# Attention and MoE on one core: from tile 16 on, probabilities are transferred into float32r buffers and transposed as float32r

## The chip, the core and the metric

The kernel runs on one core of one Trainium2 chip. A core has TensorE (PE, with its weight loads shown apart as PEld), VectorE (DVE), ScalarE (ACT), GpSimd (POOL) and SyncE (SP), which here only issues DMAs. The metric is the device time of one execution in microseconds; the median of three runs is used.

## What is computed

Attention over a window and some global positions, followed by a feed-forward part with a maximum of three products. All data are float32.

```python
# 8 batches, 8 heads, 512 local and 32 global positions, head size 64
s_g = scale * q_g @ k_all.T                       # global rows see all 544 positions
out_g = sm(s_g) @ v_all
s_ll = where(abs(i - j) <= 32, scale * q_l @ k_l.T, -1e9)
s_l = concat([scale * q_l @ k_g.T, s_ll])         # local rows: global positions and a window
out_l = sm(s_l) @ concat([v_g, v_l])
x = concat([out_g, out_l]) as (8 * 544, 512)
h = maximum(maximum(x @ w1, x @ w2), x @ w3)      # 512 -> 768
out = h @ w_out                                   # 768 -> 512
```

## The kernel before

**Tiles.** Heads go in pairs (4 pairs a batch, 32 in all), and each pair has four tiles of 128 query rows, so 128 tiles; `sl` counts tiles, `p` pairs, `t` is the tile's place in its pair. A tile sees a window of 192 or 224 keys (`WIN`), for the two heads side by side: its probabilities are a buffer of 128 partitions x 2 heads x up to 224 float32.

**One tile.** `scores` (L299) multiplies queries and keys on PE into PSUM, takes mask and minimum on DVE (L320), the exponential on ACT (L322), the reciprocal of the sum on DVE (L324, L325), and scales by it in `times` (L112 on POOL, in most cases), all in place in one buffer: `early[sl % 6]` for tiles 0 to 15, `prob[sl % 4]` from then on (L306). `trans` (L331) transposes the probabilities in four blocks of 128 x 128 on PE (L338), each with a weight load of the probabilities and the identity `ident` as the moving operand, into the PSUM tile `T`; ACT or DVE copy `T` to `pt`. `pv` (L369) multiplies `pt` by the values. The global rows of a pair go through `glob` and `glob_soft`, whose last act is six small DMAs from `sg` into `probg` (L297); `transg` (L352) transposes one block of `probg` per tile (L359).

**Two kinds of arithmetic.** Up to tile 27 (scores) and 25 (values) the matmuls are plain float32. Later ones use float32r operands, each split into a rounded part and a rest (`copy` and `sub`, L102 and L94) and multiplied in parts. Engines that write a float32r buffer round; a DMA moves bytes.

**The MoE part** of batch b - 1 is a generator (`moe_group`, L407) that emits one matmul at a time (L417 for the three products, L436 for the last one). The loop over tiles pulls 18 of them per tile with `fill`, so PE has the feed-forward of one batch between the attention of the next. Its weights are converted from a packed form during the first 26 tiles (`convert`, L155: a DMA into `wraw`, ACT L164, DVE L167 to L170, ACT L177, POOL L181); `WS` says how many steps of that stand in each tile.

**Order.** A tile's `trans` stands one tile ahead of its `pv`, and its `scores` two tiles ahead of its `trans` (L509 and after; further ahead for tiles 0 to 15). A scheduler orders the instructions of each engine from the traced program, with its own estimate of when things are ready; the transposes of tile 16 are the point behind which PE's later instructions are kept (L339 to L341). Which engine takes a copy or a scaling is decided by running sums of costs (`least`, L79). All DMAs are issued by SP in one queue, which waits in order.

**The start.** `ident` is built on POOL (L115); POOL then fills `prob`, `probg`, `qgz` and, last, `early` with zeros (L124 to L132). `early` shares its memory (tag `wol`) with a weight that is written later.

Of the kernel before, what the change touches and what calls it, by code (L numbers as in the profile page):

```python
# [9 lines left out]
F32 = mybir.dt.float32  # L10
F32R = mybir.dt.float32r
# [36 lines left out]
def f32(ap):  # L48
    return ap.bitcast(F32)


def body(ctx, tc, kin, qin, vin, min_, w1, w2, w3, w4, out):
    nc = tc.nc
    act, dve, pool, pe = nc.scalar, nc.vector, nc.gpsimd, nc.tensor

    const = ctx.enter_context(tc.tile_pool(name="const", bufs=1))
    att = ctx.enter_context(tc.tile_pool(name="att", bufs=2))
# [18 lines left out]
    def spend(e, ns):  # L76
        load[e] += ns
# [26 lines left out]
    def times(out, a, col):  # L104
        n = width(out)
        e = least({"d": n * 0.52 + 125, "a": n * 0.833 + 185, "p": n * 1.27 + 150})
        if e == "d":
            dve.tensor_scalar(out=out, in0=a, scalar1=col, scalar2=None, op0=ALU.mult)
        elif e == "a":
            act.activation(out=out, in_=a, func=AF.Copy, scale=col)  # L110
        else:
            pool.tensor_scalar(out=out, in0=a, scalar1=col, scalar2=1.0, op0=ALU.mult, op1=ALU.mult)  # L112

    ident = const.tile([128, 128], F32, name="ident")
    make_identity(nc, ident)  # L115
    mask = const.tile([128, 2, 256], BF16, name="mask")
    zero = small.tile([128, 1], F32, name="zero", bufs=1)
    dve.memset(zero, 0.0)
    prob = [const.tile([128, 2, 256], F32, name=f"prob{i}") for i in range(4)]

    probg = [const.tile([128, 3, 128], F32, name=f"probg{i}") for i in range(2)]

    qgz = const.tile([128, 2, 160], F32R, name="qgz")
    for t in (*prob, *probg):  # L124
        pool.memset(t, 0.0)
    pool.memset(f32(qgz), 0.0)

    wh = [const.tile([128, 3, 4, 128], F32R, name=f"wh{f}") for f in range(6)]
    wl = [const.tile([128, 3, 4, 128], F32R, name=f"wl{f}") for f in range(6)]

    early = const.tile([128, 6, 2, 256], F32, name="early", tag="wol")
    pool.memset(early, 0.0)  # L132
    cut = const.tile([128, 6, 512], I32, name="cut", tag="woh")
    wo = []
    xg = const.tile([128, NP, B, SG], F32, name="xg")
# [73 lines left out]
    EARLY, AHEAD = 16, 9  # L209
    kraw, kst, qraw, qs, vraw, vs, xr, sc, pg, pts = [{} for _ in range(10)]  # L210
# [73 lines left out]
    def glob_soft(p):  # L284
        if p >= B * NP:
            return
        s, nm, z = pg[p]
        dve.tensor_tensor(out=nm[:, 0:1], in0=nm[:, 0:1], in1=nm[:, 1:2], op=ALU.min)
        act.activation(out=s, in_=s, func=AF.Exp, bias=nm[:, 0:1], scale=-1.0, accum_out=z[:, 0:1])
        dve.tensor_scalar(out=z[:, 0:1], in0=z[:, 0:1], scalar1=1e-9, scalar2=None, op0=ALU.add)  # L290
        dve.reciprocal(out=z[:, 0:1], in_=z[:, 0:1])
        spend("d", 220)
        spend("a", 760)
        times(s, s, z[:, 0:1])

        for c0, n, i, h, d0 in GPUT:
            nc.sync.dma_start(out=probg[p % 2][64 * h:64 * h + 64, i, d0:d0 + n], in_=s[:, c0:c0 + n])  # L297

    def scores(sl):  # L299
        if sl >= NS:  # L300
            return
        p, t = divmod(sl, 4)
        c0, n = WIN[t]

        ps = pm.tile([128, 512], F32, name="pm") if sl < 12 else psS.tile([128, 512], F32, name="S")
        s = sc[sl] = early[:, sl % 6] if sl < EARLY else prob[sl % 4]  # L306
        nm = small.tile([128, 2], F32, name="nm")
        z = small.tile([128, 2], F32, name="z")
        ph = [ps[:, 0:224], ps[:, 224:448]]
        for j in range(2):  # L310
            if sl in NATK:

                pe.matmul(ph[j][:, 0:n], lhsT=qraw[sl][:, 128 * j:128 * j + 128], rhs=kraw[p][:, c0:c0 + n],  # L313
                          start=True, stop=True)
                continue
            for a in range(2):
                pe.matmul(ph[j][:, 0:n], lhsT=qs[sl][:, a, 128 * j:128 * j + 128],  # L317
                          rhs=kst[p][:, j, c0:c0 + n], start=(a == 0), stop=(a == 1))
        for j in range(2):
            dve.tensor_tensor_reduce(out=s[:, j, 0:n], in0=ph[j][:, 0:n], in1=mask[:, (1, 0, 1, 0)[t], 32 * (t == 0):32 * (t == 0) + n],  # L320
                                     scale=-0.125, scalar=3.0e38, op0=ALU.add, op1=ALU.min, accum_out=nm[:, j:j + 1])
            act.activation(out=s[:, j, 0:n], in_=s[:, j, 0:n], func=AF.Exp, bias=nm[:, j:j + 1], scale=-1.0,  # L322
                           accum_out=z[:, j:j + 1])
        dve.tensor_scalar(out=z, in0=z, scalar1=1e-9, scalar2=None, op0=ALU.add)  # L324
        dve.reciprocal(out=z, in_=z)  # L325
        for j in range(2):
            times(s[:, j, 0:n], s[:, j, 0:n], z[:, j:j + 1])
        spend("d", 2 * (n * 1.04 + 220) + 440)
        spend("a", 2 * (n * 0.833 + 278))

    def trans(sl):  # L331
        if sl >= NS:
            return
        s = sc.pop(sl)
        ps = psT.tile([128, 512], F32, name="T")
        for j in range(2):
            for c in range(2):
                i = pe.transpose(ps[:, 256 * j + 128 * c:256 * j + 128 * c + 128], s[:, j, 128 * c:128 * c + 128], ident)  # L338
        if sl == EARLY:  # L339

            ctx.enter_context(tc.issue_after(i.ins))  # L341
        src = ps.rearrange("p (x q) -> p x q", q=128)
        if sl < NAT:
            pt = pts[sl] = att.tile([128, 2, 2, 160], F32, name="pt", tag="pt")
            copy(pt.rearrange("p j c q -> p (j c) q")[:, :, 0:128], src, True)
        else:
            pt = pts[sl] = att.tile([128, 2, 2, 2, 160], F32R, name="pt", tag="pt")
            v = pt.rearrange("p j c a q -> p (j c) a q")
            copy(v[:, :, 0, 0:128], src, True)
            sub(v[:, :, 1, 0:128], src, f32(v)[:, :, 0, 0:128], True)  # L350

    def transg(sl):  # L352
        if sl >= NS:
            return
        p, t = divmod(sl, 4)
        pt = pts[sl]
        i, h, n = GCH[t]
        g = psS.tile([128, 512], F32, name="S")
        pe.transpose(g[:, 0:128], probg[p % 2][:, i], ident)  # L359
        src = g[:, 64 * h:64 * h + 64 * n].rearrange("p (c j g) -> p c j g", j=2, g=SG)  # L360
        if sl < NAT:
            copy(pt.rearrange("p j c q -> p c j q")[:, 0:n, :, 128:160], src, True)
            return
        v = pt.rearrange("p j c a q -> p c j a q")
        hi, lo = v[:, 0:n, :, 0, 128:160], v[:, 0:n, :, 1, 128:160]
        copy(hi, src, True)
        sub(lo, src, f32(hi), True)
# [134 lines left out]
    for sl in range(NS):  # L502
        p, t = divmod(sl, 4)
        b, n = divmod(p, NP)
# [23 lines left out]
        if sl % 16 >= 12:  # L528
            i = sl % 16 - 12
# [58 lines left out]
```

## Time and profile before

| | us |
|---|---|
| median of 3 runs | 855.65 |
| lowest and highest | 852.6 and 860.24 |
| the profiled execution | 856.24 |
| its span, first to last instruction | 854.5 |

The profile is of one execution. A span is what the instructions cover; 1.7 us of the execution's time lie around it. Where the profile names a releaser behind "<-", that is the work whose end ended a wait. Durations of PE's matmuls overlap, since they are pipelined: from the start of one to the start of the next is what one costs.

### The profile page before, as it was taken

To read this page: it belongs to the slowest core of one execution; us is meant where nothing else is said; L and a number is where in the kernel's file an instruction comes from. 1 tells how busy PE (TensorE), PEld (TensorE's weight loads), DVE (VectorE), ACT (ScalarE), POOL (GpSimd) and SP (SyncE) were. 2 spreads that over 40 slices of the span, in tenths; PEclk is the share of its full clock that TensorE was granted. 3 is DMA by queue.
4 is the path that set the end of the run, shared out by engine and by line. 5 is a ranking of instruction groups with operands and counts; after the bars stand their busy time and mean duration, and the time that the engine had idled before them with its cause. 6 is when DMAs were issued, how large, how long until landed. Compare 5 with 4: busy or idle time off the path is not lost.

```text
span 854.5 us, 15297 instructions
## 1 busy us (share of the span) xinstructions
PE 815.9 (95%) x4452; PEld 682.8 (80%) x4452; DVE 573.5 (67%) x1783; ACT 529.0 (62%) x1479; POOL 512.5 (60%) x685
## 2 busy tenths in 40 slices
PE   4867979999999999999999999999999999999997
PEld 3644757888888888888888888888888888888896
DVE  4987897676777777766777677777786776421111
ACT  3955566777677676766676776776776675511111
POOL 3865576676677566766677666866676664411211
PEclk8968999999999999999999999999999999999999
DMA  7745553232222322232223222132223211000000
GB/s 221 207 143 147 180 168 106 73 102 78 67 64 74 102 63 60 66 122 71 72 66 102 73 69 68 57 115 61 66 72 121 66 51 32 34 17 1 25 26 25
DMA packets 72420, 71.24 MB, mean 83 GB/s; under 512 B 18960, under 2 KB 63120, under 8 KB 72336
## 3 DMA queue, kind: packets, MB, share of 16 engines
q1 hardware_dynamic: 72336, 70.26, 27.7%
q8 instruction: 36, 0.59, 0.3%
q14 instruction: 48, 0.39, 0.2%
HBM read 56.85 MB, written 8.91 MB: 77 GB/s over the span
## 4 chain that ended last, share of the span: by engine, by line
PE 86%; DVE 7%; DMA 3%; ACT 2%; issue 1%; POOL 0%; SPq 0%; DVEq 0%; ACTq 0%
PE pm L417 46%; PE pm L436 17%; PE O L386 7%; PE T L338 6%; PE S L317 5%; DMA wraw<-w_in 2%; DVE wraw L169 2%; PE S L276 2%; PE S L359 2%; PE pm L313 1%; PE O L379 1%; DVE cut L170 1%; DMA wraw<-wo_in 1%; DVE cut L167 1%; DVE cut L168 1%
## 5 line engine op out<-in xcount | busy, mean ns | idle before, releaser
L417 PE MATMUL pm<-xs,wh 128*128 128x512 f32 (+1 forms) x1296 | 408.9, 388 | 2.2 <-POOL xs L94 2.2
L417 PEld LDWEIGHTS pm<-xs,wh 128*128 128x128 f32 x1296 | 234.0, 190 | 33.8 <-POOL xs L94 2.7
L417 PE MATMUL pm<-xs,wl 128*128 128x512 f32 (+1 forms) x648 | 255.5, 394 | 0.0
L417 PEld LDWEIGHTS pm<-xs,wl 128*128 128x128 f32 x648 | 122.9, 190 | 22.6 <-issue 1.8
L112 POOL TENSOR_SCALAR prob<-prob,z 128x192 f32<-128x192 f32 (+1 forms) x220 | 98.0, 458 | 66.2 <-ACT lox L102 38.2
L436 PE MATMUL pm<-woh,h 128*128 128x512 f32 x408 | 133.5, 398 | 0.0
L94 POOL TENSOR_TENSOR h<-m,h 128x512 fp32r<-128x512 f32 (+1 forms) x54 | 68.3, 1265 | 100.1 <-ACT h L102 100.1
L425 DVE TENSOR_TENSOR m<-pm,m 128x512 f32<-128x512 f32 (+1 forms) x108 | 71.2, 659 | 70.6 <-PE pm L417 69.6
L322 ACT ACTIVATE prob<-prob,nm 128x192 f32<-128x192 f32 (+1 forms) x224 | 103.3, 462 | 16.1 <-DVE nm L320 13.7
L94 POOL TENSOR_TENSOR qs<-qraw,qs 128x256 fp32r<-128x256 f32 x100 | 73.5, 744 | 63.9 <-ACT qs L102 62.5
L94 DVE TENSOR_TENSOR pt<-T,pt 128x512 fp32r<-128x512 f32 x102 | 70.5, 691 | 58.8 <-ACT pt L102 58.0
L324 DVE TENSOR_SCALAR z<-z 128x2 f32<-128x2 f32 x128 | 53.1, 415 | 50.5 <-ACT prob L322 48.7
L436 PEld LDWEIGHTS pm<-woh,h 128*128 128x128 f32 x408 | 74.8, 189 | 11.5
L436 PE MATMUL pm<-wol,h 128*128 128x512 f32 x204 | 82.5, 405 | 0.0
L102 ACT CAST pt<-T 128x512 fp32r<-128x512 f32 x90 | 52.8, 587 | 45.5 <-PE T L338 43.9
L94 POOL TENSOR_TENSOR vs<-vraw,vs 128x256 fp32r<-128x256 f32 x102 | 75.5, 740 | 9.0 <-ACT vs L102 4.8
L320 DVE CUSTOM_DVE_ANT_0 prob<-S,mask 128x192 f32<-128x192 f32 (+1 forms) x224 | 74.8, 371 | 6.7 <-PE S L313 4.1
L94 POOL TENSOR_TENSOR kst<-kraw,kst 64x576 fp32r<-64x576 f32 x49 | 70.5, 1439 | 11.1 <-issue 7.8
L102 ACT CAST qs<-qraw 128x256 fp32r<-128x256 f32 x100 | 40.7, 407 | 55.7 <-PE S L317 54.2
L386 PEld LDWEIGHTS O<-pt,vs 128*128 128x128 f32 x408 | 66.2, 188 | 8.3
L386 PE MATMUL O<-pt,vs 128*128 128x320 f32 (+1 forms) x408 | 72.7, 299 | 0.0
L338 PEld LDWEIGHTS T<-ident,prob 128*128 128x128 f32 x448 | 56.0, 141 | 15.0 <-POOL prob L112 0.2
(99 smaller groups left out, 1351.7 us busy)
## 6 DMA issues: line engine op xcount, KB each, us to landing
vraw<-v_in SPq DMA_DIRECT2D x128, 128.0 KB, 2.1
qraw<-q_in SPq DMA_DIRECT2D x100, 128.0 KB, 2.2
wraw<-w_in SPq DMA_DIRECT2D x18, 512.0 KB, 4.2
out_dram<-o SPq DMA_DIRECT2D x32, 256.0 KB, 2.5
kraw<-k_in SPq DMA_DIRECT2D x25, 320.0 KB, 3.0
qn<-q_in SPq DMA_DIRECT2D x28, 128.0 KB, 2.7
wraw<-wo_in SPq DMA_DIRECT2D x6, 512.0 KB, 3.7
probg<-sg SPq DMA_DIRECT2D x96, 24.0 KB, 1.9
```

Source lines behind the costliest of these rows:

```text
L94: (dve if least(c) == "d" else pool).tensor_tensor(out=out, in0=a, in1=b, op=ALU.subtract)
L102: act.copy(out=out, in_=a)
L112: pool.tensor_scalar(out=out, in0=a, scalar1=col, scalar2=1.0, op0=ALU.mult, op1=ALU.mult)
L317: pe.matmul(ph[j][:, 0:n], lhsT=qs[sl][:, a, 128 * j:128 * j + 128], rhs=kst[p][:, j, c0:c0 + n], start=(a == 0), stop=(a == 1))
L320: dve.tensor_tensor_reduce(out=s[:, j, 0:n], in0=ph[j][:, 0:n], in1=mask[:, (1, 0, 1, 0)[t], 32 * (t == 0):32 * (t == 0) + n], scale=-0.12 ...
L322: act.activation(out=s[:, j, 0:n], in_=s[:, j, 0:n], func=AF.Exp, bias=nm[:, j:j + 1], scale=-1.0, accum_out=z[:, j:j + 1])
L324: dve.tensor_scalar(out=z, in0=z, scalar1=1e-9, scalar2=None, op0=ALU.add)
L338: i = pe.transpose(ps[:, 256 * j + 128 * c:256 * j + 128 * c + 128], s[:, j, 128 * c:128 * c + 128], ident)
L386: pe.matmul(o[:, j, 0:320].rearrange("p (a q) -> p a q", a=2)[:, :, 0:n], lhsT=vs[sl][:, 2 * j + c].rearrange("p a d -> p (a d)"), rhs=pt[ ...
L417: pe.matmul(ps[:, 0:n], lhsT=w[f][:, i, k], rhs=xs[k][:, a, 0:n], start=(q == 0), stop=(q == 11))
L425: dve.tensor_tensor(out=m[:, 0:n], in0=ps[:, 0:n], in1=m[:, 0:n], op=ALU.max)
L436: pe.matmul(ps, lhsT=hh[f][:, a, 128 * t:128 * t + 128], rhs=w[:, f], start=(q == 0), stop=(q == 17))
```

## The change

Three things are changed.

1. From tile 16 on, the softmax of a tile runs in a plain float32 buffer `s` (four of them, in turn). A DMA on SP's queue then moves the scaled probabilities into one of two float32r buffers `prob`. The transposes read `prob` as float32r, with an identity `identr` in float32r, and write a float32r view of the PSUM tile `T`.
2. The global rows' buffers `probg` become float32r, and their 128 transposes too; their DMAs stay as they are. Tiles 0 to 15 still transpose float32 in place.
3. To make room, `ident` moves into the sixth part of `early`, which leaves five parts for the tiles 0 to 15. `early` is now filled with zeros first, and two buffers `prob` in place of four after it. `identr` is a copy of `ident` made by DVE.

```diff
-    ident = const.tile([128, 128], F32, name="ident")
+    early = const.tile([128, 6, 2, 256], F32, name="early", tag="wol")
+    ident = early[:, 5, 0, 0:128]
     make_identity(nc, ident)
+    identr = const.tile([128, 128], F32R, name="identr")
+    dve.tensor_copy(out=identr, in_=ident)
...
-    prob = [const.tile([128, 2, 256], F32, name=f"prob{i}") for i in range(4)]
-    probg = [const.tile([128, 3, 128], F32, name=f"probg{i}") for i in range(2)]
+    prob = [const.tile([128, 2, 256], F32R, name=f"prob{i}") for i in range(2)]
+    probg = [const.tile([128, 3, 128], F32R, name=f"probg{i}") for i in range(2)]
     qgz = const.tile([128, 2, 160], F32R, name="qgz")
-    for t in (*prob, *probg):
-        pool.memset(t, 0.0)
-    pool.memset(f32(qgz), 0.0)
+    pool.memset(early[:, 0:5], 0.0)
+    for t in (*prob, *probg, qgz):
+        pool.memset(f32(t), 0.0)
...
-    early = const.tile([128, 6, 2, 256], F32, name="early", tag="wol")
-    pool.memset(early, 0.0)
...
-        s = sc[sl] = early[:, sl % 6] if sl < EARLY else prob[sl % 4]
+        if sl < EARLY:
+            s = sc[sl] = early[:, sl % 5]
+        else:
+            s = att.tile([128, 2, 224], F32, name="s", bufs=4)
+            sc[sl] = prob[sl % 2]
...
+        if sl >= EARLY:
+            nc.sync.dma_start(out=f32(sc[sl])[:, :, 0:n], in_=s[:, :, 0:n])
...
+        pr, one = (ps, ident) if sl < EARLY else (ps.bitcast(F32R), identr)
         for j in range(2):
             for c in range(2):
-                i = pe.transpose(ps[:, 256 * j + 128 * c:256 * j + 128 * c + 128], s[:, j, 128 * c:128 * c + 128], ident)
+                i = pe.transpose(pr[:, 256 * j + 128 * c:256 * j + 128 * c + 128], s[:, j, 128 * c:128 * c + 128], one)
...
-        pe.transpose(g[:, 0:128], probg[p % 2][:, i], ident)
+        pe.transpose(g.bitcast(F32R)[:, 0:128], probg[p % 2][:, i], identr)
```

The scheduler is given another program, so rows move. Line numbers of the changed kernel are a little higher: L320 becomes L325, L338 becomes L346, L417 becomes L425, and so on; a number behind a name is a buffer's.

PE, in the stretch where a batch's feed-forward runs beside the next batch's attention, around the transposes of one tile with t = 1. Before:

```order
L417 MATMUL pm<-xs,wl_112 128x512
L338 MATMUL T<-ident,prob_93 128x128 x4
L417 MATMUL pm<-xs,wh_107 128x512 x2
L417 MATMUL pm<-xs,wl_113 128x512
L417 MATMUL pm<-xs,wh_107 128x512
L317 MATMUL S<-kst,qs 128x224 x4
```

and after:

```order
L425 MATMUL pm<-xs,wl_111 128x512
L346 MATMUL T<-identr,prob_93 128x128 x4
L425 MATMUL pm<-xs,wh_106 128x512 x2
L425 MATMUL pm<-xs,wl_112 128x512
L425 MATMUL pm<-xs,wh_106 128x512
L322 MATMUL S<-kst,qs 128x224 x4
```

Nothing moved there: four transposes stand between the same matmuls, in another type and from another buffer.

SP's queue in the same stretch, one pair of heads: queries (`qraw`), values (`vraw`), keys (`kraw`) and the six transfers of the global rows. Before:

```order
L297 DMA probg_94<-sg 64x64
L240 DMA qraw<-q_in 128x256
L252 DMA vraw<-v_in 128x256
L240 DMA qraw<-q_in 128x256
L252 DMA vraw<-v_in 128x256 x2
L240 DMA qraw<-q_in 128x256 x2
L252 DMA vraw<-v_in 128x256
L218 DMA kraw<-k_in 128x640
```

and after:

```order
L298 DMA probg_95<-sg 64x64
L241 DMA qraw<-q_in 128x256
L334 DMA prob_93<-s 128x2x224
L253 DMA vraw<-v_in 128x256
L241 DMA qraw<-q_in 128x256
L334 DMA prob_92<-s 128x2x224
L253 DMA vraw<-v_in 128x256
L334 DMA prob_93<-s 128x2x192
L253 DMA vraw<-v_in 128x256
L241 DMA qraw<-q_in 128x256 x2
L334 DMA prob_92<-s 128x2x192
L219 DMA kraw<-k_in 128x640
```

Four transfers a pair have come in, one for each tile; the loads stand among themselves as they did.

DVE, first rows of the program: `mask` is the cast of the mask, L280 the minimum of the global rows, L167 to L169 the first weight conversion, L320 the minimum of a tile. Before:

```order
L484 CAST mask<-cut 128x2x224
L280 ISA sg,nmg<-S,zero 64x384
L280 ISA nmg 64x1
L280 ISA sg,nmg<-S,zero 64x160
L280 ISA nmg 64x1
L288 TENSOR_TENSOR nmg<-nmg 64x1
L290 TENSOR_SCALAR zg<-zg 64x1
L291 RECIPROCAL zg<-zg 64x1
L167 TENSOR_SCALAR cut<-cut 128x512
L168 TENSOR_SCALAR cut<-cut 128x512
L169 SCALAR_TENSOR_TENSOR wraw<-wraw,cut 128x512
L320 ISA early,nm<-pm,mask 128x192
```

and after:

```order
L492 CAST mask<-cut 128x2x224
L281 ISA sg,nmg<-S,zero 64x384
L281 ISA nmg 64x1
L325 ISA early,nm<-pm,mask 128x192
L325 ISA nm 128x1
L325 ISA early,nm<-pm,mask 128x192
L325 ISA nm 128x1
L325 ISA early,nm<-pm,mask 128x224
L325 ISA nm 128x1
L325 ISA early,nm<-pm,mask 128x224
L325 ISA nm 128x1
L281 ISA sg,nmg<-S,zero 64x160
```

The first tiles' minima have moved ahead of the rest of the global rows and of the first weight conversion, which in the changed program stands behind the minima of eight tiles. On PE, ACT, POOL and SP the order differs likewise up to about tile 28; from there on it is the same but for the new transfers and a few swapped neighbours on DVE.

More of the change, by code (lines that the diff above doesn't have):

```diff
@@ L296, in glob_soft @@
         for c0, n, i, h, d0 in GPUT:
-            nc.sync.dma_start(out=probg[p % 2][64 * h:64 * h + 64, i, d0:d0 + n], in_=s[:, c0:c0 + n])
+            nc.sync.dma_start(out=f32(probg[p % 2])[64 * h:64 * h + 64, i, d0:d0 + n], in_=s[:, c0:c0 + n])
     def scores(sl):
```

## The prediction, made before the change was run

> **What bounds the kernel now.** I read the page first (busy time, then the chain that ended last), then the busy time by stage, then the instructions of TensorE (PE) around one tile, and last the first 20 us.
>
> ```profile
> span 854.5 us, 15297 instructions
> PE 815.9 (95%) x4452; PEld 682.8 (80%) x4452; DVE 573.5 (67%) x1783; ACT 529.0 (62%) x1479; POOL 512.5 (60%) x685
> PE 86%; DVE 7%; DMA 3%; ACT 2%; issue 1%; POOL 0%; SPq 0%; DVEq 0%; ACTq 0%
> ...
> 0.00:20.00 20.00, 9.06 (x28) 6.67 (x29) 7.80 (x34) 6.54 (x19) 7.11 (x16) 0.86 0.74 228
> 20.00:149.00 129.00, 106.32 (x600) 78.54 (x599) 110.24 (x296) 86.87 (x249) 88.27 (x96) 0.89 0.53 159
> 149.00:745.00 596.00, 595.81 (x3262) 506.69 (x3263) 438.01 (x1421) 418.44 (x1179) 400.84 (x557) 1.00 0.25 74
> 745.00:854.00 109.00, 104.75 (x565) 90.91 (x564) 17.42 (x34) 17.13 (x33) 16.31 (x17) 1.00 0.06 20
> ```
>
> In the stage rows the columns are the stretch, its length, the busy time of PE, weight load, VectorE (DVE), ScalarE (ACT) and GpSimd (POOL), the granted clock, the DMA share and GB/s. From 149 to 745 us PE is busy 595.81 of 596.00 at clock 1.00, while DVE has 438.01 and POOL 400.84: there PE alone sets the pace, and the other engines have room. The chain of the whole run is 86% PE. Before 149 us PE has holes; after 745 us there are no tiles left, and the change does not reach it. So a cheaper PE instruction counts in full between 149 and 745 us, and work on another engine counts only if PE comes to wait for it.
>
> **The four transposes of a tile.** This is PE in order of time around one tile; columns are start, length of the merged group, and what it is:
>
> ```profile
> 402.06 0.39 PE L417 MATMUL pm<-xs,wl 128*128 128x512 f32 x1
> 402.29 0.60 PE L338 MATMUL T<-ident,prob 128*128 128x128 f32 x4
> 402.65 0.70 PE L417 MATMUL pm<-xs,wh 128*128 128x512 f32 x2
> 403.19 0.39 PE L417 MATMUL pm<-xs,wl 128*128 128x512 f32 x1
> 403.42 0.40 PE L417 MATMUL pm<-xs,wh 128*128 128x512 f32 x1
> 403.65 0.59 PE L317 MATMUL S<-kst,qs 128*128 128x192 f32 x4
> 415.62 0.60 PE L317 MATMUL S<-kst,qs 128*128 128x224 f32 x4
> ```
>
> A float32r matmul of 512 columns takes 0.23 us (403.19 to 403.42, 403.42 to 403.65). From 402.29 to 403.19 stand four transposes and two such matmuls: 0.90 - 0.46 = 0.44, so 0.11 us for each transpose of 128 columns. At the matmul's rate 128 columns would take 0.23 / 4 = 0.058. What holds the transpose at 0.11? Either its own passes, or the load of the next weights. Groups by line and shape, the last numbers being busy time and mean ns of one (the first two rows from 105 to 145 us, the others from 400 to 440 us):
>
> ```profile
> L313 PE MATMUL S<-kn,qn 128*128 128x224 f32 x12 | 2.8, 352 | 0.0
> L313 PE MATMUL S<-kn,qn 128*128 128x192 f32 x12 | 2.4, 325 | 0.0
> ...
> L386 PE MATMUL O<-pt,vs 128*128 128x320 f32 x19 | 4.2, 307 | 0.0
> L386 PE MATMUL O<-pt,vs 128*128 128x256 f32 x6 | 1.6, 278 | 0.0
> L338 PE MATMUL T<-ident,prob 128*128 128x128 f32 x28 | 4.2, 272 | 0.0
> ...
> L317 PEld LDWEIGHTS S<-kst,qs 128*128 128x128 f32 x28 | 4.2, 190 | 0.6
> L338 PEld LDWEIGHTS T<-ident,prob 128*128 128x128 f32 x28 | 3.5, 140 | 0.9
> ```
>
> L313 multiplies plain float32: 32 columns more cost 352 - 325 = 27 ns, 0.84 ns a column. L386 multiplies float32r: 64 columns more cost 29 ns, 0.45 a column, about half. Carried down to 128 columns, the float32 line gives 325 - 64 x 0.84 = 271, and the transpose measures 272: it streams like any float32 matmul, twice per column. In float32r it should stream in 0.058 us. The weight load speaks against this being all: in the seven rows above, four L317 matmuls take 0.59 with 192 columns and 0.60 with 224, so those go at the pace of their weight loads, about 0.11. But the load of a transpose is shorter, 140 ns against 190, by 50 ns; taken off that pace of 0.11 it leaves some 0.06. So neither the load nor the stream need hold a float32r transpose above 0.06.
>
> The rule that speaks against it: the Trainium skill, "TensorE: Matmul & The Clock Gate", section "LDWEIGHTS (loading the stationary operand)", has the load's time as the number of columns over 1.2, 107 ns for 128 columns whatever the type. By that rule the 0.11 of now is the load's, and this term is zero. The 140 against 190 is against it; no row of this case shows a float32r transpose.
>
> **The change, part by part.**
>
> *Transposes from tile 16 (L338).* Of a tile's four, the first three are followed by a short load and gain 0.110 - 0.058 = 0.052; the fourth is followed by the full load of the next matmul, 0.11, and gains nothing. That is 0.156 us a tile. Tiles 26 to 127 stand in the stretch where PE alone counts: 102 x 0.156 = **-15.9**. Ends: 0 if the load or the number of passes stays, -15.9 if both are as above; I take the full value, since both rows nearest to it say so.
>
> *Transposes of the global rows (L359), 128.* Each stands alone between two wide matmuls and is followed by a full load of 0.11: **0**. The cover is that load; without it they would gain another 0.05 each.
>
> *Transfer of each tile from 16 on, 112 more DMAs on SP's queue.* What a tile's transposes wait for now is the end of the scaling by POOL; then comes the transfer. Landing time is bounded by the rows of the page on either side in size (the last number is us from issue to landing):
>
> ```profile
> qraw<-q_in SPq DMA_DIRECT2D x100, 128.0 KB, 2.2
> kraw<-k_in SPq DMA_DIRECT2D x25, 320.0 KB, 3.0
> ```
>
> A tile is 192 or 224 KB, so 2.5 to 2.6 as an estimate between these. The room, from the end of scaling to the transposes, is seen in pairs of rows, POOL then PE: a usual tile, the tightest kind, and tiles 16 and 17:
>
> ```profile
> 407.39 0.83 POOL L112 TENSOR_SCALAR prob<-prob,z 128x192 f32<-128x192 f32 x2 [0.42 <-DVE z L325]
> 414.26 0.60 PE L338 MATMUL T<-ident,prob 128*128 128x128 f32 x4
> ...
> 270.37 0.83 POOL L112 TENSOR_SCALAR prob<-prob,z 128x192 f32<-128x192 f32 x2
> 274.10 0.27 PE L338 MATMUL T<-ident,prob 128*128 128x128 f32 x1
> ...
> 75.95 0.83 POOL L112 TENSOR_SCALAR prob<-prob,z 128x192 f32<-128x192 f32 x2 [2.97 <-DVE z L325]
> 77.63 0.60 PE L338 MATMUL T<-ident,prob 128*128 128x128 f32 x4
> 79.18 0.88 POOL L112 TENSOR_SCALAR prob<-prob,z 128x224 f32<-128x224 f32 x2 [0.39 <-DVE z L325]
> 79.85 0.70 PE L338 MATMUL T<-ident,prob 128*128 128x128 f32 x4
> ```
>
> The usual tile has 414.26 - 408.22 = 6.04: hidden. The tightest has 274.10 - 271.20 = 2.90, less 0.31 because PE reaches it two tiles' savings earlier, 2.59 against 2.5. It comes once in 16 tiles, behind the splitting of a batch's attention output on POOL, six times from tile 31 to 111. At a landing of 3.0 each would cost 0.41, 2.5 in all; at 2.5 nothing: I take **+0.6**. Tile 16 has 0.85 and tile 17 none: late by 1.65 and 2.6, up to 4.3; or nothing, if other work holds that stretch, where PE has holes anyway. I take the middle, **+2.1**.
>
> *SP's queue.* The transfer waits for its scaling, and the loads behind it wait with it. The worst place is the tile behind the six global transfers:
>
> ```profile
> 416.31 3.66 SPq L297 DMA_DIRECT2D probg<-sg  x6
> 418.64 0.88 POOL L112 TENSOR_SCALAR prob<-prob,z 128x224 f32<-128x224 f32 x2 [0.40 <-ACT vs L102]
> 420.07 0.53 SPq L240 DMA_DIRECT2D qraw<-q_in  x1
> 425.65 0.60 PE L338 MATMUL T<-ident,prob 128*128 128x128 f32 x4
> ```
>
> SP is free at 420.60, 1.1 after the scaling; landing at 423.2 leaves 2.4 to 425.65. Queued behind it are loads for later tiles: **0**. DMA has room: its share there is 0.25, and 23.9 MB come on top of 71.24.
>
> *Two buffers in place of four.* A transfer must wait for the transposes two tiles back, which PE issues before this tile's scores: **0**. DVE's few swapped rows: **0**, covered by its 158 us of room.
>
> *The start.* GpSimd fills fewer zeros and `early` is cleared first; what counts is that DVE's first rows come in another order.
>
> ```profile
> 6.92 0.53 DVE L280 CUSTOM_DVE_ANT_0 sg<-S,zero 64x384 f32<-64x384 f32 x1
> 14.37 0.43 DVE L167 TENSOR_SCALAR cut<-cut 128x512 f32<-128x512 f32 x1 [4.02 <-ACT cut L164]
> 15.90 0.35 DVE L320 CUSTOM_DVE_ANT_0 early<-pm,mask 128x192 f32<-128x192 f32 x1
> ```
>
> Now tile 0's softmax stands behind the first weight conversion, which waits 4.02 us for its data; after the change it follows L280 at about 7.4 us, 8.5 earlier, and DVE was idle 12.2 of the first 20 us. Against it, the first conversion moves behind eight tiles' minima: 16 x 0.35 = 5.6 and the small rows between, so some 16 us in place of 14.37, and DVE, which does the conversions, is the busiest engine beside PE up to 149 us. Ends: -8.5 and +1.6; I take **-3**, nearly the middle, on the side of the gain because idle time is filled.
>
> *Sum.* -15.9 + 0.6 + 2.1 - 3 = -16.2 on the profiled execution's 856.24: 840.0. The median of the three runs, 855.65, lies 0.6 lower, so **839.4**.
>
> **The rivals.**
> - *The transposes keep 0.11*: their load takes the full 0.11 in float32r, as L317's does, or a transpose of four-byte data passes twice in any case. For it: L317 shows a float32r floor at 0.11; against it: the load of 140 ns. Then -16.2 + 15.9 - 0.3 (the tight tiles keep 2.90): 855.0 against the median. A chance of 0.36.
> - *They fall half-way*, to about 0.083, because stream and load overlap imperfectly: 3 x 0.027 x 102 = 8.3 in place of 15.9, so 847.0. No row shows such a middle value. 0.14.
> - *Slower: the transfer comes late in the steady stretch.* Its place is SP's queue, where a load with a longer wait stands ahead of it. The price is one for one for each tile late. To end 1% above before (8.6) it must undo 16.2 as well: 24.8 / 102 = 0.24 us a tile, when landing plus queue pass 6.0 us from the scaling. The rows above show 3.7 at the worst usual place. At 0.35 a tile: 875. 0.08.
>
> **How the numbers follow.** My forecast (transposes at about 0.058) has 0.42 and a range of its own of 831 to 848: the start's ends and the two late tiles around 839.4. Low end for all: 831; about 0.04 lies under it. High end: 860, which leaves out the slower rival and some 0.05 of the unchanged one. A measurement of this kernel can tell about 1% from no change, its three runs spreading from 852.6 to 860.24. Faster by over 1% (under 847.1): 0.40 of the forecast, 0.08 of the half-way case, 0.03 of the unchanged one: 0.51. Slower (over 864.2): 0.08 + 0.01 = 0.09. The rest, 0.40, is the same.
>
> **What would show it.** In the profile after: transposes from tile 16 with a mean near 220 ns instead of 272, and from their start to the matmul after next about 0.74 instead of 0.90; their load still 140. If the load shows 190, the first rival holds. PE's idle time in front of a transpose, put down to the transfer into the new buffers, tells the slower one; it should stand at tiles 16 and 17 alone and a little at tile 31 and every 16th after it. DVE's first tile should start near 7.4 us, and PE's stretch without holes should begin near 148 instead of 149 us; if that comes later than 152, the start was misjudged.

## The result and the profile after

| | before | after |
|---|---|---|
| median of 20 runs, us | 859.4 | 851.03 |
| lowest and highest | 852.6 and 861.52 | 849.77 and 855.34 |
| the profiled execution | 856.24 | 852.36 |
| its span | 854.5 | 850.6 |

The ratio is 0.9923, with a 95% interval of 0.9905 to 0.994: 6.6 us less (5.2 to 8.2). The means of the twenty runs differ by 6.6 too, the medians by 8.4, since some runs of the kernel before lie far under its median; the two profiled executions differ by 3.9, the one of before being among its faster ones. The time lies in the predicted range of 831 to 860, far above its value of 839.4, and the gain of over 1%, which had the greater chance, did not come. The twenty runs put the kernel before at 859.4; the three shown beforehand had come out low, at 855.65. Measured against 859.4 the prediction's -16.2 would have been 843.2. So the gain was 0.4 of what was forecast by the ratio, and half of it by the medians.

The page of the changed kernel, its first lines and the chain that ended last:

```profile
span 850.6 us, 15712 instructions
PE 811.6 (95%) x4452; PEld 674.6 (79%) x4452; DVE 566.0 (67%) x1784; ACT 527.9 (62%) x1479; POOL 510.0 (60%) x683
...
PE 87%; DVE 5%; DMA 2%; issue 2%; ACT 2%; SPq 1%; POOL 0%; DVEq 0%; ACTq 0%; POOLq 0%
```

Its busy time by stage (stretch, length, PE, weight load, DVE, ACT, POOL, granted clock, DMA share, GB/s):

```profile
0.00:20.00 20.00, 12.96 (x51) 9.00 (x51) 9.14 (x58) 11.22 (x39) 10.14 (x24) 0.99 0.63 200
20.00:149.00 129.00, 101.78 (x562) 73.86 (x562) 97.69 (x271) 80.94 (x226) 78.27 (x84) 0.88 0.58 177
149.00:745.00 596.00, 596.00 (x3296) 504.08 (x3296) 442.26 (x1424) 419.65 (x1185) 405.24 (x560) 1.00 0.37 111
```

Three things can be read there. In the first 20 us PE does 12.96 us of work where it did 9.06. From 20 to 149 us it does less than before, 101.78 against 106.32, with SP's queue (SPq) now in the chain. From 149 to 745 us it is as full as it was, with the transfers on top: DMA 0.37 in place of 0.25.

The span splits well at two points that all kernels of this study have: the start of the first transpose of tile 28, from which PE has almost no holes, and that of tile 127. Starts in the profiled executions:

| first transpose of | before | after |
|---|---|---|
| tile 0 | 19.32 | 13.36 |
| tile 16 | 77.63 | 74.69 |
| tile 28 | 162.94 | 165.05 |
| tile 127 | 740.30 | 736.53 |
| the 99 tiles between the last two | 577.36 | 571.48 |

The start gains 6.0, which is all lost again by tile 28 (2.1 behind), and the steady part, the 99 tiles, gains 5.9, or 0.059 a tile. The forecast had 0.156 a tile.

The transposes of one tile, PE and then its weight loads (start, length of the merged group):

```profile
401.74 0.40 PE L425 MATMUL pm<-xs,wl 128*128 128x512 f32 x1
401.98 0.46 PE L346 MATMUL T<-identr,prob 128*128 128x128 f32 x4
402.27 0.70 PE L425 MATMUL pm<-xs,wh 128*128 128x512 f32 x2
402.81 0.40 PE L425 MATMUL pm<-xs,wl 128*128 128x512 f32 x1
```

```profile
401.74 0.55 PEld L346 LDWEIGHTS T<-identr,prob 128*128 128x128 f32 x4
402.24 0.30 PEld L425 LDWEIGHTS pm<-xs,wh 128*128 128x128 f32 x2
```

From the first transpose to the matmul after next it is 402.81 - 401.98 = 0.83, where it was 0.90 and 0.74 was forecast. The four transposes and the load behind them cost 0.83 - 0.46 = 0.37 in place of 0.44. The loads show the pace. The first starts early, at 401.74, beside the matmul ahead; the single records of the other three start at 401.979, 402.065 and 402.151, the next full load at 402.236, the one behind it at 402.345. So a transpose's load is followed after 0.086, a full one after 0.109. Before, the same four starts were 402.296, 402.404, 402.512 and 402.622, 0.109 apart: three steps of a tile gain 0.023 each. Groups by shape, 400 to 440 us (last: busy time, mean ns of one):

```profile
L346 PE MATMUL T<-identr,prob 128*128 128x128 f32 x28 | 3.2, 238 | 0.0
...
L367 PE MATMUL S<-identr,probg 128*128 128x128 f32 x7 | 1.6, 222 | 0.0
```

```profile
L322 PEld LDWEIGHTS S<-kst,qs 128*128 128x128 f32 x28 | 4.2, 189 | 0.6
L346 PEld LDWEIGHTS T<-identr,prob 128*128 128x128 f32 x28 | 3.2, 141 | 0.9
```

A lone float32r transpose (L367) now has 222 ns, the value forecast for a single pass, where the float32 one had 272. In a row (L346) the mean is 238, and the load still reads 141 against 189. So the type did what was expected of the stream, and in a row the load of a transpose did not follow 50 ns sooner than a full one: 0.086 against 0.109, 23 ns apart.

What PE waited for from 20 to 149 us, first after and then before (in total, times, longest):

```profile
PE S L367 <- DMA probg<-sg: 10.1, 4, 4.5
PE O L387 <- ACT pt L102: 5.1, 7, 1.3
PE T L346 <- DMA prob<-s: 4.7, 4, 1.9
```

```profile
PE S L359 <- DMA probg<-sg: 7.1, 3, 4.9
PE S L359 <- DVE nm L320: 5.4, 3, 2.4
```

The transfers are waited for four times, 4.7 us, and the small transfers of the global rows longer than before.

### The profile page after: what moved, and what is told of

Same layout as the page of the kernel before. It is cut to its first block, busy times and chain, and to the rows that moved or that the text cites. A ratio compares the mean times of both kernels' runs of the same rounds, so it can differ in the third digit from the quotient of the medians.

```text
span 850.6 us, 15712 instructions
## 1 busy us (share of the span) xinstructions
PE 811.6 (95%) x4452; PEld 674.6 (79%) x4452; DVE 566.0 (67%) x1784; ACT 527.9 (62%) x1479; POOL 510.0 (60%) x683
## 4 chain that ended last, share of the span: by engine, by line
PE 87%; DVE 5%; DMA 2%; issue 2%; ACT 2%; SPq 1%; POOL 0%; DVEq 0%; ACTq 0%; POOLq 0%
PE pm L425 48%; PE pm L444 17%; PE O L394 7%; PE S L322 5%; PE T L346 4%; PE S L277 2%; PE O L387 1%; DVE wraw L170 1%; DMA wraw<-w_in 1%; PE S L367 1%; PE pm L318 1%; PE S L318 1%; DVE cut L169 1%; DVE cut L168 1%; PE S L273 0%
## 5 line engine op out<-in xcount | busy, mean ns | idle before, releaser
L425 PE MATMUL pm<-xs,wh 128*128 128x512 f32 (+1 forms) x1296 | 409.4, 389 | 0.8 <-POOL xs L94 0.8
L425 PEld LDWEIGHTS pm<-xs,wh 128*128 128x128 f32 x1296 | 234.2, 190 | 32.8 <-POOL xs L94 1.2
L425 PE MATMUL pm<-xs,wl 128*128 128x512 f32 (+1 forms) x648 | 254.1, 392 | 0.0
L112 POOL TENSOR_SCALAR s<-s,z 128x192 f32<-128x192 f32 (+1 forms) x220 | 101.6, 474 | 67.0 <-ACT lox L102 36.5
L425 PEld LDWEIGHTS pm<-xs,wl 128*128 128x128 f32 x648 | 123.0, 190 | 23.5 <-issue 2.4
L327 ACT ACTIVATE s<-s,nm 128x192 f32<-128x192 f32 (+1 forms) x224 | 103.1, 461 | 9.1 <-DVE nm L325 6.9
L329 DVE TENSOR_SCALAR z<-z 128x2 f32<-128x2 f32 x128 | 54.9, 429 | 48.7 <-ACT s L327 47.6
L444 PEld LDWEIGHTS pm<-woh,h 128*128 128x128 f32 x408 | 74.6, 188 | 11.6
L325 DVE CUSTOM_DVE_ANT_0 s<-S,mask 128x192 f32<-128x192 f32 (+1 forms) x224 | 74.7, 371 | 12.0 <-PE S L318 5.5
L346 PEld LDWEIGHTS T<-identr,prob 128*128 128x128 f32 x448 | 50.8, 141 | 20.6 <-ACT xr L102 2.3
```

Source lines behind the costliest of these rows:

```text
L346: i = pe.transpose(pr[:, 256 * j + 128 * c:256 * j + 128 * c + 128], s[:, j, 128 * c:128 * c + 128], one)
L425: pe.matmul(ps[:, 0:n], lhsT=w[f][:, i, k], rhs=xs[k][:, a, 0:n], start=(q == 0), stop=(q == 11))
L444: pe.matmul(ps, lhsT=hh[f][:, a, 128 * t:128 * t + 128], rhs=w[:, f], start=(q == 0), stop=(q == 17))
```

## The experiments

The first question is which part of the change brought what: type, transfer, or start. The theory by then was that a row of transposes goes at the pace of its weight loads, 0.086, and that the early transfers, of tiles 16 to 25, eat the gain of the start. "Stretch" is the time from tile 28's first transpose to tile 127's.

**The type taken back.** All buffers, transfers and the start stay, but every transpose is float32 again.

```diff
-        pr, one = (ps, ident) if sl < EARLY else (ps.bitcast(F32R), identr)
+        one = ident if sl < EARLY else f32(identr)
+        if sl >= EARLY:
+            s = f32(s)
...
-        pe.transpose(g.bitcast(F32R)[:, 0:128], probg[p % 2][:, i], identr)
+        pe.transpose(g[:, 0:128], f32(probg[p % 2])[:, i], f32(identr))
```

> The changed kernel with its transfers, buffers and start, but all transposes in plain float32 again. Yardstick: from the first transpose of tile 28 to that of tile 127, 577.4 us before and 571.5 after the change. Theory (the gain is the transposes' alone, the weight loads between them coming every 0.086 us in place of 0.109, and the transfers cost nothing in the steady stretch): that stretch goes back to 577.4 (within 0.5), and the time is that of before within 3 us, whatever the start brings. Rival (the gain is the start's, or the transfers give back part of what the transposes save): the time stays 5 us or more under before, or the stretch comes out over 578.

Measured: 856.62, ratio to before 0.9979 [0.9954, 1.0003]; the stretch 577.50 against 577.36 before. The type is what shortens the stretch, by 6.0, and nothing else in the change touches it: the transfers cost nothing there.

**The transfer taken away.** The scaling writes the float32r buffer itself.

```diff
-            times(s[:, j, 0:n], s[:, j, 0:n], z[:, j:j + 1])
-        if sl >= EARLY:
-            nc.sync.dma_start(out=f32(sc[sl])[:, :, 0:n], in_=s[:, :, 0:n])
+            times(sc[sl][:, j, 0:n], s[:, j, 0:n], z[:, j:j + 1])
```

> The changed kernel without the 112 transfers: from tile 16 on the scaling writes the float32r buffers itself, which rounds the probabilities. Theory: the stretch from tile 28 to 127 stays 571.5 (within 0.5), since the transfers are hidden there; only tiles 16 to 25 gain, so the time is 0 to 5 us under that of the changed kernel, a ratio to before of 0.986 to 0.993. Rival (the transfers give back some of the saving in the steady stretch): the stretch falls to 569 or less.

Measured: 846.53, 0.9846 [0.9819, 0.9873]; the stretch 571.52, as after the change (571.48). Against the 851.03 of the changed kernel, on another chip, the transfers cost some 4.5 us. Tile 28's first transpose comes at 159.82 in place of 165.05 and the stretch is the same, so all of it lies ahead of tile 28.

**The start alone.** The kernel before with `early` cleared first, five parts of it, the identity inside, and a float32 copy of that for the tiles from 16 on.

```diff
-    ident = const.tile([128, 128], F32, name="ident")
+    early = const.tile([128, 6, 2, 256], F32, name="early", tag="wol")
+    ident = early[:, 5, 0, 0:128]
...
+    pool.memset(early[:, 0:5], 0.0)
...
-        s = sc[sl] = early[:, sl % 6] if sl < EARLY else prob[sl % 4]
+        s = sc[sl] = early[:, sl % 5] if sl < EARLY else prob[sl % 4]
```

> The kernel before with the changed start alone: early filled with zeros first and in five parts, the identity inside it, a copy of the identity for later; transposes and buffers as before. Theory: DVE's first minimum of a tile near 7.4 us in place of 15.9, but little of it is left by 149 us; the stretch is 577.4, the time within 3 us of before. Rival (the start is what brings the gain): 5 to 8 us less than before, ratio 0.991 to 0.994.

Measured: 853.57, 0.993 [0.9906, 0.9955], on a chip where before had 859.24: 5.7 us less by the medians. The theory's bound of 3 us was wrong here, and the rival's range was met. The kernel's first rows of DVE show the move (start, length, what):

```profile
6.49 0.53 DVE L282 CUSTOM_DVE_ANT_0 sg<-S,zero 64x384 f32<-64x384 f32 x1
...
7.07 0.36 DVE L322 CUSTOM_DVE_ANT_0 early<-pm,mask 128x192 f32<-128x192 f32 x1
```

Tile 0's minimum starts at 7.07 in place of 15.90. Tile 0's first transpose comes at 12.59, 6.7 earlier than before, tile 28's at 159.43, 3.5 earlier, and the stretch is 577.36, to the hundredth that of before. So by the two traces half of the start's gain is kept, 3.5 us. They do not explain the rest of the 5.7. The trace of before is one of its faster executions (856.24, at a granted clock of 0.980), while on this chip the runs of before have a clock of 0.973 in the median and those of the start alone 0.983. Whether the start raises the clock stays open.

What the changed kernel loses ahead of tile 28 is not the start's: the kernel with the transfers but without the type, on the same chip, has 3.05 us more than this one (856.62 - 853.57).

**Transposes apart.** One MoE matmul between each two transposes of a tile, so that each is followed by a full load.

```diff
+                if sl > EARLY and (j, c) != (1, 1):
+                    fill(1)
...
-        fill(4)
+        fill(1 if sl >= EARLY else 4)
```

> The changed kernel with a tile's four transposes set apart, from tile 17 on: one matmul of the feed-forward between each two, so that each is followed by a full weight load. Theory (what follows a transpose is held by the next weight load, 0.11 for a full one and 0.086 for a transpose's): a lone transpose costs 0.114 as in plain float32, four cost 0.456 in place of 0.369, and the stretch grows by 99 x 0.087 = 8.6 to 580. Rival (the transpose's own stream is what costs): no change, 571.5 within 1.

Measured: 868.11, 1.009 [1.0061, 1.012]. PE around one tile:

```profile
404.26 0.22 PE L346 MATMUL T<-identr,prob 128*128 128x128 f32 x1
404.32 0.45 PE L427 MATMUL pm<-xs,wh 128*128 128x512 f32 x1
404.60 0.22 PE L346 MATMUL T<-identr,prob 128*128 128x128 f32 x1
404.66 0.45 PE L427 MATMUL pm<-xs,wh 128*128 128x512 f32 x1
404.95 0.22 PE L346 MATMUL T<-identr,prob 128*128 128x128 f32 x1
```

A transpose and a matmul take 0.34 to 0.35; less 0.23 for the matmul that is 0.11, as the theory has it. Note where it is spent: the matmul starts 0.06 behind the transpose, the stream's time, and its successor 0.28 behind it. The stream is over early; the record of the matmul behind it lasts 0.45, where the same matmul elsewhere has 0.40. That fits a wait for the load of its full weight, which the trace does not name. But the stretch grew to 586.49, 15.0 over the changed kernel instead of the 8.6 expected. The single pace is confirmed; the size of the whole is not. The other matmuls of a tile stand otherwise too, and the waits that the trace names in the stretch, 2.4 us in all, do not make up the 6.4 that are over: what does stays open.

**Transposes doubled.** From tile 17 on each transpose runs twice. This kernel was executed once.

```diff
-                i = pe.transpose(pr[:, 256 * j + 128 * c:256 * j + 128 * c + 128], s[:, j, 128 * c:128 * c + 128], one)
+                for _ in range(2 if sl > EARLY else 1):
+                    i = pe.transpose(pr[:, 256 * j + 128 * c:256 * j + 128 * c + 128], s[:, j, 128 * c:128 * c + 128], one)
```

> The changed kernel with every float32r transpose of a tile issued twice from tile 17 on, the second writing the same block again: eight in a row where four stood. Theory (a transpose in a row is held by its weight load at 0.086 us): four more cost 4 x 0.086 = 0.344 a tile, so the stretch from the first transpose of tile 28 to that of tile 127 grows from 571.5 by 34 to 605.5. Rival (a transpose in a row costs its stream of 128 columns, 0.058, as predicted): it grows by 23 to 594.5. At the 0.109 of plain float32 it would be 43 more.

Measured: 887.08, stretch 605.15. Over 571.48 that is 33.7 us for 99 x 4 more transposes, 0.085 each. In the trace:

```profile
404.63 0.81 PE L347 MATMUL T<-identr,prob 128*128 128x128 f32 x8
405.28 0.69 PE L426 MATMUL pm<-xs,wh 128*128 128x512 f32 x2
405.81 0.40 PE L426 MATMUL pm<-xs,wl 128*128 128x512 f32 x1
```

From 404.63 to 405.81, eight transposes and two matmuls, it is 1.18 in place of 0.83: 0.0875 for each of the four added, with ends rounded to 0.01. So a transpose in a row costs 0.085 to 0.088, in rows of four as in rows of eight.

**The early transfers taken away, or kept without a reader.** Tiles 16 to 25 get their rounded probabilities by the scaling, as in the kernel without transfers; the transfer stands from tile 26 on (`NAT`). The second kernel also puts a transfer that nobody reads at the place of each early one, from the new buffer back into the old. Both ran on two chips, the second time beside the changed kernel.

```diff
-            times(s[:, j, 0:n], s[:, j, 0:n], z[:, j:j + 1])
-        if sl >= EARLY:
+            times(sc[sl][:, j, 0:n] if EARLY <= sl < NAT else s[:, j, 0:n], s[:, j, 0:n], z[:, j:j + 1])
+        if sl >= NAT:
             nc.sync.dma_start(out=f32(sc[sl])[:, :, 0:n], in_=s[:, :, 0:n])
+        elif sl >= EARLY:
+            nc.sync.dma_start(out=s[:, :, 0:n], in_=f32(sc[sl])[:, :, 0:n])
```

(The last two lines stand in the second kernel only.)

> The changed kernel with transfers only from tile 26 on; for tiles 16 to 25 the scaling writes the float32r buffers itself, which rounds their probabilities. Theory (the transfers cost something only in tiles 16 to 25, where the weight conversions hold the pace): as without any transfer, 846 to 848, ratio 0.983 to 0.987. Rival (the later 102 transfers cost too): 849 to 851, ratio 0.989 to 0.992.

> As the kernel with transfers from tile 26 on, but tiles 16 to 25 have a transfer of the same size at the same place in SP's queue that no transpose waits for (from the scaled buffer back into the buffer of the softmax). Theory Q (what the ten early transfers cost is that weight loads stand behind them in SP's queue): the cost is back, 850 to 852. Theory L (it is the landing that transposes of tiles 16 to 25 wait for): 846 to 848, as without them.

> The changed kernel itself, on the same chip as the three that follow: 850 to 852.

> Transfers only from tile 26 on, tiles 16 to 25 with rounded probabilities, once more: 846 to 848.5, 3 to 5 us under the changed kernel on the same chip.

> The ten early transfers in SP's queue with nobody waiting for them, once more (tiles 16 to 25 with rounded probabilities). Theory Q (weight loads stand behind them in the queue): within 1 us of the changed kernel. Theory L (transposes wait for the landing): within 1 us of the kernel without early transfers. The first run stood between the two.

| | first chip | ratio to before | second chip | ratio to before |
|---|---|---|---|---|
| changed kernel | | | 851.75 | 0.9924 [0.9896, 0.9952] |
| no early transfer | 847.97 | 0.986 [0.9835, 0.9886] | 846.98 | 0.9872 [0.9841, 0.9904] |
| early transfer, unread | 850.28 | 0.989 [0.9859, 0.9922] | 849.99 | 0.991 [0.9881, 0.9938] |

The early transfers cost 4.8 us (851.75 - 846.98). Of that, 3.0 (2.3 on the first chip) come although no transpose waits for their data, with intervals that overlap on either chip. On the first chip the time is in the range of theory Q (the queue); on the second it stands between the two theories. What such transfers do is hold SP's queue, which waits at each for the scaling. The waits of SP's queue in the changed kernel, 20 to 149 us, and two pieces of its chain:

```profile
SPq L334 <- POOL s L112: 22.1, 8, 6.6
```

```profile
82.33 1.18 POOL s L112 x2
83.52 0.63 SPq L334
84.25 0.55 SPq L219
...
85.87 6.65 DMA wraw<-w_in
...
105.78 0.61 SPq L334
106.44 0.61 SPq L298
...
108.38 1.81 DMA probg<-sg
...
110.28 0.34 PE S L367
```

At tile 18 the queue stands until the scaling ends, then come three loads of attention data, and behind them the load of packed weights, which lands at 92.5 and on which the conversion waits. At tile 21 the small transfers of the global rows stand behind the tile's transfer, and PE waits for them. The last weight load shows how late the queue runs. Without early transfers, then with unread ones:

```profile
140.52 0.33 SPq L160 DMA_DIRECT2D wraw<-wo_in  x1
```

```profile
149.28 0.37 SPq L160 DMA_DIRECT2D wraw<-wo_in  x1
```

Nearly 9 us later with nothing but unread transfers in the queue; 147.15 in the changed kernel, 139.29 before. Where PE loses its time is another matter. Starts in one execution of each kernel on the second chip:

| first transpose of | no early transfer | unread | changed |
|---|---|---|---|
| tile 16 | 71.48 | 71.10 | 73.38 |
| tile 19 | 89.28 | 88.86 | 93.63 |
| tile 22 | 114.54 | 114.67 | 120.01 |
| tile 28 | 158.61 | 158.36 | 163.97 |
| tile 30 | 170.25 | 172.10 | 175.59 |
| the stretch | 572.38 | 574.75 | 572.21 |

With unread transfers PE reaches tile 28 no later than without any, however late the weights come; its loss, 2.4, lies in the stretch, most of it by tile 30 (on the first chip 159.65 against 160.73, and 574.24 against 572.13). The changed kernel is 5.4 late at tile 28, all of that by tile 22, and loses nothing behind it. So the 4.8 cannot be split into 3.0 for the queue and 1.8 for the wait on the data. That the queue alone costs 2 to 3 us is what the times on both chips say; what the changed kernel loses, it loses in another place, and that loss comes only with transposes that wait for the transfers. Up to 149 us its PE waits 3.9 us for their landings, where the kernel without early transfers waits for none, and 11.2 for the small transfers of the global rows against 5.6 there. How much of the latter is the queue's was not separated. A landing can also take long: that of tile 19, issued beside loads of packed weights. The changed kernel's first profile, 84 to 96 us (KB each, us from issue to landing):

```profile
wraw<-w_in SPq DMA_DIRECT2D x3, 512.0 KB, 7.1
...
prob<-s SPq DMA_DIRECT2D x1, 192.0 KB, 7.5
```

**The early transfers issued by POOL.** The ten early transfers leave SP's queue.

```diff
-            nc.sync.dma_start(out=f32(sc[sl])[:, :, 0:n], in_=s[:, :, 0:n])
+            (pool if sl < NAT else nc.sync).dma_start(out=f32(sc[sl])[:, :, 0:n], in_=s[:, :, 0:n])
```

> The changed kernel with the ten transfers of tiles 16 to 25 issued by POOL, which does most of the scaling, in place of SP: nothing stands behind them in SP's queue, but the transposes still wait for the landing. Theory Q: 846 to 848.5, as without early transfers. Theory L: 850 to 852, as changed.

Measured: 858.52, 0.9991 [0.9968, 1.0015], 6.8 us above the changed kernel on the same chip. SP's queue is free of them, yet tile 28 comes at 171.76, and the time is that of neither theory. The trace shows DVE's weight conversions longer; the changed kernel (its run beside this one) and this one, 70 to 160 us, ten steps each (busy time, mean ns of one):

```profile
L170 DVE SCALAR_TENSOR_TENSOR wraw<-wraw,cut 128x512 int32<-128x512 int32 x10 | 9.3, 934 | 0.2
L171 DVE SCALAR_TENSOR_TENSOR cut<-wraw 128x512 int32<-128x512 int32 x10 | 8.2, 818 | 0.0
L169 DVE TENSOR_SCALAR cut<-cut 128x512 int32<-128x512 int32 x10 | 7.4, 738 | 0.1
L168 DVE TENSOR_SCALAR cut<-cut 128x512 f32<-128x512 f32 x10 | 6.4, 642 | 5.0 <-ACT cut L165 5.0
```

```profile
L170 DVE SCALAR_TENSOR_TENSOR wraw<-wraw,cut 128x512 int32<-128x512 int32 x10 | 11.0, 1100 | 0.1
L171 DVE SCALAR_TENSOR_TENSOR cut<-wraw 128x512 int32<-128x512 int32 x10 | 9.9, 992 | 0.0
L168 DVE TENSOR_SCALAR cut<-cut 128x512 f32<-128x512 f32 x10 | 9.6, 960 | 2.9 <-ACT cut L165 2.9
L169 DVE TENSOR_SCALAR cut<-cut 128x512 int32<-128x512 int32 x10 | 6.5, 646 | 0.1
```

37.0 us in place of 31.3, one L168 among them of 3.79 us (most others there have 0.4), which began 0.2 ahead of such an issue on POOL. The kernel before has one of 3.45 us too, at 100.17, without any DMA from POOL. Whether the issuing itself slows DVE, or only that POOL's and DVE's rows came to lie otherwise, was not separated. As a way out of the queue it failed.

**The switch at tile 26.** Tiles 16 to 25 keep plain float32 transposes in two buffers of their own; from tile 26 on the changed kernel's way. The probabilities are not rounded.

```diff
+    plain = [const.tile([128, 2, 256], F32, name=f"plain{i}") for i in range(2)]
...
+        elif sl < NAT:
+            s = sc[sl] = plain[sl % 2]
...
-        if sl >= EARLY:
+        if sl >= NAT:
             nc.sync.dma_start(out=f32(sc[sl])[:, :, 0:n], in_=s[:, :, 0:n])
```

> The changed kernel with the switch to transfers and float32r transposes at tile 26 in place of tile 16; tiles 16 to 25 use two plain float32 buffers of their own and transpose them in float32 in place. Nothing is rounded. Theory (the three parts add: start -5.7, float32r transposes in the steady stretch -5.9, no early transfers): 847 to 849, ratio 0.985 to 0.988. Rival (the ten early tiles gain something by float32r as well, or the parts do not add): 850 to 852.

Measured: 847.08 (846.79 to 848.98), 0.9855 [0.983, 0.988], 13.5 us under the 860.57 of before on that chip. Tile 28's first transpose stands at 159.78, the stretch is 572.46: the start's gain and the type's, without the loss between. The two parts give -11.6 (-5.7 and -5.9), so about 2 more came than they account for. It beats both kernels.

## Why the prediction was wrong, step by step

**Transposes from tile 16.** This is the step that failed, and its mechanism was half right. The stream did fall to one pass (222 ns alone). The step that failed is the sentence that takes the 50 ns between two records of a load off the pace of 0.11 and gets 0.06. A record's length is not the distance to the next: loads of 190 ns follow each other at 0.109, those of 141 at 0.086. So three steps of a tile gain 0.023 each, not 0.052, 0.07 a tile; the whole stretch shows 0.059 a tile, -5.9 in the 99 tiles and some -6.1 for 102, against -15.9. The first rival, an unchanged 0.11, is refuted by the stretch; the half-way one, at 0.083, is close to what happened, though it was set aside because no row showed a middle value. Whether its reason holds, stream and load overlapping imperfectly, stays open: rows of eight keep the pace of rows of four, as they would with a load of its own speed and as they would with a fixed loss in the overlap.

The rule weighed there, from the Trainium skill, "TensorE: Matmul & The Clock Gate", section "LDWEIGHTS (loading the stationary operand)", has the columns over 1.2, so 107 ns for 128 columns. For full loads the trace agrees: 0.109. For the loads of float32r transposes it does not: 0.086, in one kernel with rows of four and in another with rows of eight, and here the measurement decides. By the rule the type would have brought nothing; it brought 6.

**Global rows' transposes.** Zero, as forecast. Alone, a transpose costs 0.11 in either type, since the full load behind it does.

**Transfers.** In the steady part they cost nothing, right: stretches with and without them are 571.48 and 571.52. The tight tiles were given 0.6 and cost nothing. One of them, tile 47, POOL, SP's queue and PE in order:

```profile
271.45 0.83 POOL L112 TENSOR_SCALAR s<-s,z 128x192 f32<-128x192 f32 x2
272.31 0.61 SPq L334 DMA_DIRECT2D prob<-s  x1
275.11 0.46 PE L346 MATMUL T<-identr,prob 128*128 128x128 f32 x4
```

The scaling ends at 272.28, the transfer is issued 0.03 later and takes 2.3 us by the page (`prob<-s` of 192 KB; 2.4 for 224 KB, where 2.5 to 2.6 was estimated): 274.6, half a microsecond in hand. Landings among the weight loads were not so short: up to 7.5.

**Tiles 16 and 17.** The 2.1 was the price of PE waiting for two landings. Those waits are there, with two more, at tiles 19 and 23:

```profile
74.69 0.50 PE L346 MATMUL T<-identr,prob 128*128 128x128 f32 x4 [1.91 <-DMA prob<-s]
78.92 0.51 PE L346 MATMUL T<-identr,prob 128*128 128x128 f32 x4 [1.31 <-DMA prob<-s]
94.78 0.51 PE L346 MATMUL T<-identr,prob 128*128 128x128 f32 x4 [1.32 <-DMA prob<-s]
128.14 0.51 PE L346 MATMUL T<-identr,prob 128*128 128x128 f32 x4 [0.20 <-DMA prob<-s]
```

Together they are 4.7, over twice the 2.1. Tiles 19 and 23 were not priced, and every landing was taken at 3.0 or less, where tile 19's took 7.5. In all the changed kernel is 5.2 later at tile 28 than the kernel without transfers (165.05 - 159.82), so 2.1 was too small by about 3.

**SP's queue.** Given nothing, from a row at 416 us, and right for that stretch. It was never looked at for the tiles 16 to 25, where the queue also feeds the weight conversion and the global rows. Transfers that nobody reads cost 2.3 to 3.0 there; how much of the changed kernel's 4.8 is the queue's is not shown.

**Two buffers, DVE's swaps.** Nothing of either is seen: the stretch without type is that of before.

**The start.** -3 was taken between -8.5 and +1.6; alone it brings -3.5 by the traces, close to that, and -5.7 by the medians. DVE's first tile was forecast near 7.4 us and comes at 6.96 in the changed kernel, 7.07 with the start alone. In the changed kernel the early transfers take this gain away again, and its profile alone looks as if the start had brought nothing. The sign named for it, where PE's stretch without holes begins, misleads too: the last hole ends at 144.7 us, earlier than before (149.2), but PE has done less by then, 562 records from 20 to 149 us against 600. When a given tile starts is the better sign.

**The sum.** By the traces: -3.5 for the start, +5.6 for what the changed kernel has lost against it by tile 28 (165.05 - 159.43), -5.9 for the type, -3.8 in all; the two spans differ by 3.9. By the medians: -5.7 for the start and +4.8 for early transfers, with the -5.9 of the traces, -6.8; measured -6.6 by the ratio and -8.4 by the medians. Either way the type's term is what the forecast missed most, by 10 us.

## What to carry to other kernels

The pace of a queue of short instructions is read from the starts of consecutive ones, not from the lengths of their records; where no row shows the new instruction, the half-way case deserves more than a small chance. A transfer put between two engines has to be costed in every stage it passes: its landing beside the other loads there, and what stands behind it in a queue that waits in order. Where an early cost shows is read from the starts of tiles, since the same total can be lost in another place. A cheaper instruction should be switched on only from the place on where its engine is what is waited for. Gains and losses that lie in different stages are told apart by one kernel per stage: here the start, measured alone, was worth nearly as much as the whole change (ratios of 0.993 and 0.9923).

## What the runs showed of the hardware

- Weight loads of float32r transposes follow each other at 0.085 to 0.088 us, full loads in a row and those of float32 transposes at 0.109, at the granted clock of 1.00. A float32 transpose has a load of the same record length as a float32r one, so it is not the record that tells the pace; two passes would give about 0.108 as an estimate (128 columns x 0.84 ns, measured from 105 to 145 us at a clock of 0.96).
- The steady stretch hardly differs between executions: 577.36, 577.36 and 577.50 in three kernels with float32 transposes, 571.48 and 572.21 in two executions of the changed one, while the twenty runs of before spread over 9 us. Those runs were not traced, but the longer of them have the lower granted clock, as on the second chip (852.74 at 0.982, 861.09 at 0.972), and in the trace of before the clock is under 1.00 only ahead of 149 us (0.86 and 0.89). That fits a spread from what lies ahead of the stretch.
- Ten transfers issued by POOL instead of SP came with weight conversions on DVE that took 37.0 us for ten steps in place of 31.3, and with 6.8 us more in all; why was not settled.
- A transfer of 192 KB from `s` to `prob` took 2.3 us from issue to landing in the median, and 7.5 beside three loads of 512 KB, where the DMA share was 0.82 (84 to 96 us).
